# Summing the expert counts one background step later in the gates of the attention layer with experts

## The chip, the cores and the metric

The kernel runs on one core of one Trainium2 chip. The metric is the device time of one execution in microseconds (us), without the host. Three runs of the kernel before gave 539.40, 538.65 and 539.07 us; their median is 539.07 us.

## The reference

Three layers follow each other in fp32, on 4 batches of 576 positions: a linear attention, a layer in which two of four attention experts answer each position, and a layer of eight feed-forward experts.

```python
def _attn_ref(q, k, v, w_phi):              # layer 1: 8 heads, 128 features
    def phi(x):
        proj = np.einsum('bhsd,df->bhsf', x, w_phi)
        proj = proj - np.max(np.abs(proj), axis=-1, keepdims=True)
        return np.concatenate([np.exp(proj), np.exp(-proj)], axis=-1)
    q_p, k_p = (phi(q), phi(k))
    kv = np.einsum('bhsf,bhsd->bhfd', k_p, v)
    z = np.sum(k_p, axis=2)
    num = np.einsum('bhsf,bhfd->bhsd', q_p, kv)
    den = np.einsum('bhsf,bhf->bhs', q_p, z)[..., None] + 1e-06
    return (num / den).astype(np.float32)

def _moe_ref(x, w_gate, wq, wk, wv, wo):    # layer 2: E = 4 attention experts, K = 2
    logits = x @ w_gate
    topk = np.argpartition(-logits, K, axis=-1)[..., :K]
    sel = np.take_along_axis(logits, topk, axis=-1)
    w = np.exp(sel - sel.max(-1, keepdims=True))
    w /= w.sum(-1, keepdims=True) + 1e-09
    for e in range(E):
        q, k, v = x @ wq[e], x @ wk[e], x @ wv[e]
        ...                                 # causal softmax a of scale * q k^T
        ye = a @ v @ wo[e]
        for kk in range(K):
            out += (topk[:, :, kk] == e)[..., None] * w[:, :, kk:kk + 1] * ye

def _moe2_ref(x, w_gate, w_local, w1, w2):  # layer 3: E = 8, F = 1024
    ...                                     # each position keeps the expert of the one before, or takes a fresh one
    out[b, s] = p[e] * (np.maximum(x[b, s] @ w1[e], 0.0) @ w2[e])
```

## The kernel before

**Phase A** (class `PhaseA`) is layer 1. It runs 16 units (4 batches by 4 pairs of heads) in a software pipeline, by the list `A_STEPS`: `k`, `e`, `q` project keys and queries (tiles pjk, pje, pjq, line 267), `x` and `f` transpose and take exponentials, `kv` multiplies keys by values (Y, L335), `s` sums the keys (L344), `n0` and `n1` give the numerators (pn, L384), `d0` and `d1` in every second unit the denominators (pd, L401). `n0` is copied out of its accumulator by VectorE (DVE, L389), `n1` by ScalarE (ACT, L387), the denominators by DVE (L403).

**Phase B** (classes `PhaseB` and `Slot`) is layer 2. Each batch has a slot (s0, s1, s2, s3) for the two experts that its positions use most, and a fifth slot, x, takes one further expert. `B_STEPS` lists the steps of a slot: `s` scores (sc), `p` transposes, `v`, `o` the output projection (px, L64 to L66, copied out by ACT in L1238), `f` or `h` one of the next slot's (or its own remaining) projections (pq, twelve matmuls in L770). A projection's two halves are written by ACT as the high part (L735, two instructions) and subtracted by DVE as the low part (L737, two instructions); the values' half is copied by ACT alone (L753). **Phase C** is layer 3.

**The gates of layer 2** (`Gates.top2`, line 535) run once for each batch, as a generator in the background queue (class `Background`). A `t` in a step list is a tick, and a tick takes one step of the first entry of each lane; the gates are in lane "r". A bare `yield` ends a step and the next one comes with the next tick; `yield 2` lets one tick pass without a step, `yield 3` two. The steps of `top2` that matter here, each in terms of its lines:

- the counts: the selection `sel` (L557, L558), a memset (L559) and `cnt`, the sum over the five groups of positions (L561), on DVE;
- the sum of the counts over the partitions: a matmul with a matrix of ones (pc, L564; two matmul instructions of 4 columns), and in the same step five DVE instructions that scale the weights `w` (L565, L567 to L570);
- the total `tot`, which reads the matmul's accumulator on DVE (L574);
- the ranks (`by_use`, L522 and L524): how many experts have a larger total; then `hot` (L527), and then `perm` (L530, L532).

For the batches in turn, counted through the lists: the first batch's counts stand in unit 9 after `f0`, its pc between `kv1` and `kv2`, its total after `kv3`. The second batch's pc stands in unit 13 between `z0` and `s0`, its total after `d1`. The third's pc stands at the first tick of slot s0, ahead of `s0a s0b h1`, its total after them. The fourth's pc stands in slot x ahead of `f f p0a`, its total after them.

**What sets the order.** The program text does not give the order on an engine by itself. A planner goes through the program with modelled times and gives each engine, whenever it comes free, the earliest instruction in the text that is ready in the model; the engines then run the order that came out. A step of the background queue may not be issued ahead of the anchors, the last marked instructions of the main work on the same engine (`Background.step`, `issue_after`). pc, pje, pn, pd, the gates' logits pg (L503), pq and px share one tag of accumulators, `mm`, with two buffers:

```python
            ps.same = {"tr": ("X", 5), "X": ("X", 5), "mm": ("mm", 2)}
```

A tile of the tag needs one of the two buffers, and a buffer comes free when the last reader of its tile is done; pc's last reader is `tot`.

Of the kernel before, what the change touches and what calls it, by code (L numbers as in the profile page):

```python
# [484 lines left out]
class Gates:  # L485
# [5 lines left out]
    def t(self, shape, tag, b, bufs=1, dt=F32):  # L491
        return self.wk.tile([128] + list(shape), dt, tag=tag, name=f"{tag}_{b}", bufs=bufs)
# [42 lines left out]
    def top2(self, xf, wg32, b, out):  # L535

        nc, k, t, ps = self.nc, self.k, self.t, self.ps
        L = t([QT, 4], "L4", b)
        nc.vector.memset(L[:, 4, :], 0.0)
        yield from self.logits(xf, wg32, 4, L, b)  # L540
        Le = L[:, :, :, None].to_broadcast([128, QT, 4, 4])
        Lf = L[:, :, None, :].to_broadcast([128, QT, 4, 4])

        mx = t([QT], "mx", b)
        nc.vector.tensor_reduce(mx, L, axis=AX.X, op=OP.max)
        w = t([QT, 4], "w4", b)
        nc.vector.tensor_tensor(w, L, mx[:, :, None].to_broadcast([128, QT, 4]), op=OP.subtract)
        nc.scalar.activation(w, w, AF.Exp)
        yield
        c1, c2 = t([QT, 4, 4], "c1", b), t([QT, 4, 4], "c2", b)  # L550
        nc.vector.tensor_tensor(c1, Lf, Le, op=OP.is_gt)
        nc.vector.tensor_tensor(c2, Lf, Le, op=OP.is_equal)
        nc.vector.tensor_tensor(c2, c2, k.lower[:, None, 0:4, 0:4].to_broadcast([128, QT, 4, 4]), op=OP.mult)
        nc.vector.tensor_tensor(c1, c1, c2, op=OP.add)
        yield
        sel = t([QT, 4], "sel", b)
        nc.vector.tensor_reduce(sel, c1, axis=AX.X, op=OP.add)  # L557
        nc.vector.tensor_scalar(sel, sel, 1.5, None, op0=OP.is_lt)  # L558
        nc.vector.memset(sel[64:128, 4, :], 0.0)  # L559
        cnt = t([4], "cnt4", b)  # L560
        nc.vector.tensor_reduce(cnt, sel.rearrange("p t e -> p e t"), axis=AX.X, op=OP.add)  # L561
        yield 2
        pc = ps.tile([128, HALF], F32, tag="mm", name=f"pc_{b}")
        nc.tensor.matmul(pc[:, 0:4], k.ones, cnt, start=True, stop=True)  # L564
        nc.vector.tensor_tensor(w, w, sel, op=OP.mult)  # L565
        sm = t([QT], "sm", b)
        nc.vector.tensor_reduce(sm, w, axis=AX.X, op=OP.add)  # L567
        nc.vector.tensor_scalar(sm, sm, 1e-9, None, op0=OP.add)
        nc.vector.reciprocal(sm, sm)
        nc.vector.tensor_tensor(w, w, sm[:, :, None].to_broadcast([128, QT, 4]), op=OP.mult)  # L570
        yield
        tot = t([4], "tot4", b)

        nc.vector.scalar_tensor_tensor(tot, pc[:, 0:4], 8.0, k.iota[:, 0:4], op0=OP.mult, op1=OP.subtract)  # L574
        yield
        yield from self.by_use(tot, 4, b)
        hot, perm = self.hot, self.perm
        yield

        t4 = t([QT, 4, 4], "c1", b)  # L580
        nc.vector.tensor_tensor(t4, w[:, :, None, :].to_broadcast([128, QT, 4, 4]),
                                hot[:, None, :, :].to_broadcast([128, QT, 4, 4]), op=OP.mult)
        ws = t([QT, 4], "ws", b, 4)
        nc.vector.tensor_reduce(ws, t4, axis=AX.X, op=OP.add)
        out.update(ws=ws, perm=perm, hot=hot, tot=tot)
        yield
# [1209 lines left out]
```

## Time and profile before

| | |
|---|---|
| median of three runs | 539.07 us |
| the profiled execution's own time | 539.2 us |
| its span, first to last instruction | 537.0 us |
| TensorE matmul (PE) busy | 515.2 us (96%) |
| VectorE (DVE) busy | 359.2 us (67%) |
| ScalarE (ACT) busy | 264.9 us (49%) |
| GpSimd (POOL) busy | 150.2 us (28%) |

The profile is one execution. PE is TensorE's matmuls, PEld its weight loads. A line of the timeline gives the start, the time covered, the engine, the line of the kernel with its operation and tiles, and the count; in brackets stand idle time of the engine just ahead and what ended it. Lines of one kind that follow each other are merged.

### The profile page before, as it was taken

The page shows a single profiled execution, that of the slowest core. Times are in us where ns is not written, and L with a number is a line of the kernel's source. Part 1 is how long each engine was busy: PE and PEld are TensorE (multiplying, and loading weights), DVE is VectorE, ACT ScalarE, POOL GpSimd, SP SyncE. Part 2 cuts the span into 40 slices and gives each one's busy share as a digit, 9 for nine tenths or more (in the row PEclk, how much of TensorE's full clock was granted, in tenths as well). Part 3 has the DMA queues.
Part 4 walks back from the last instruction along what each step waited for, and adds up shares of the span by engine and source line. Part 5 has one row for each costly group of instructions (what it writes and reads, how often), then busy time and mean ns, then how long its engine had stood idle before and what let it go on. Part 6 is the DMA issues. An engine that isn't in the chain of part 4 may idle for free.

```text
span 537.0 us, 11793 instructions
## 1 busy us (share of the span) xinstructions
PE 515.2 (96%) x4456; PEld 435.4 (81%) x4456; DVE 359.2 (67%) x968; ACT 264.9 (49%) x607; POOL 150.2 (28%) x254
## 2 busy tenths in 40 slices
PE   7999999999999999999899899999999999999995
PEld 5776765666666787778677798999999999999995
DVE  7776777878863787877897965742764366617541
ACT  3857566565665467867748455331451235115100
POOL 5674696398467141212016100000000000000000
PEclk9999999999999999999999999999999999999998
DMA  8433364444116024602003202081435133813011
GB/s 249 134 98 105 108 215 126 149 147 164 28 44 212 9 69 131 196 2 81 1 0 139 100 1 69 13 287 75 134 144 169 46 129 123 282 48 128 2 57 38
DMA packets 32709, 57.07 MB, mean 106 GB/s; under 512 B 7012, under 2 KB 17636, under 8 KB 31620
## 3 DMA queue, kind: packets, MB, share of 16 engines
q1 hardware_dynamic: 32644, 56.24, 32.2%
q8 instruction: 37, 0.61, 0.5%
q14 instruction: 28, 0.23, 0.1%
HBM read 41.86 MB, written 14.36 MB: 105 GB/s over the span
## 4 chain that ended last, share of the span: by engine, by line
PE 83%; DVE 9%; ACT 4%; DMA 1%; issue 1%; SPq 0%; POOL 0%; DVEq 0%; ACTq 0%; POOLq 0%
PE po_c L64 6%; PE po_c L65 6%; PE po_c L66 6%; PE ph_c L64 6%; PE ph_c L65 6%; PE pq_s L770 6%; PE ph_c L66 6%; PE Y L335 6%; PE pn L384 5%; PE pd L401 3%; PE pjk L267 3%; PE py_s L917 2%; PE pt_s L889 2%; PE tr L321 2%; PE pjq L267 2%; PE pg L503 2%
## 5 line engine op out<-in xcount | busy, mean ns | idle before, releaser
L1478 ACT ACTIVATE h_c<-ph_c 128x288 fp32r<-128x288 f32 x64 | 26.0, 410 | 104.0 <-PE ph_c L66 103.9
L64 PE MATMUL ph_c<-xh_c,w1h_c 128*128 128x288 f32 x256 | 76.9, 301 | 0.0
L64 PE MATMUL po_c<-h_c,w2h_c 128*128 128x288 f32 x256 | 76.1, 297 | 0.0
L65 PE MATMUL po_c<-h_c,w2h_c 128*128 128x288 f32 x256 | 75.5, 295 | 0.0
L65 PE MATMUL ph_c<-xl_c,w1h_c 128*128 128x288 f32 x256 | 75.5, 295 | 0.0
L66 PE MATMUL po_c<-h_c,w2l_c 128*128 128x288 f32 x256 | 75.4, 295 | 0.0
L66 PE MATMUL ph_c<-xh_c,w1l_c 128*128 128x288 f32 x256 | 75.3, 295 | 0.0
L311 POOL TENSOR_TENSOR zs<-a_kp 128x256 f32<-128x256 f32 x64 | 48.2, 766 | 51.8 <-ACT a_kp L307 25.9
L1479 DVE SCALAR_TENSOR_TENSOR h_c<-ph_c,h_c 128x288 fp32r<-128x288 f32 x64 | 28.6, 452 | 34.5 <-ACT h_c L1478 34.2
L64 PEld LDWEIGHTS ph_c<-xh_c,w1h_c 128*128 128x128 f32 x256 | 48.1, 188 | 1.9 <-issue 0.9
L64 PEld LDWEIGHTS po_c<-h_c,w2h_c 128*128 128x128 f32 x256 | 48.1, 188 | 0.9 <-issue 0.9
L65 PEld LDWEIGHTS ph_c<-xl_c,w1h_c 128*128 128x128 f32 x256 | 48.1, 188 | 0.0
L66 PEld LDWEIGHTS po_c<-h_c,w2l_c 128*128 128x128 f32 x256 | 48.1, 188 | 0.0
L66 PEld LDWEIGHTS ph_c<-xh_c,w1l_c 128*128 128x128 f32 x256 | 48.0, 188 | 0.1
L65 PEld LDWEIGHTS po_c<-h_c,w2h_c 128*128 128x128 f32 x256 | 48.1, 188 | 0.0
L770 PE MATMUL pq_s<-xh_b,w_s 128*128 128x288 f32 x192 | 43.5, 304 | 0.7 <-DVE b_kz L737 0.3
L1501 DVE TENSOR_TENSOR fo_c<-po_c,pb 128x288 f32<-128x288 f32 x32 | 14.5, 454 | 44.3 <-PE po_c L66 44.2
L335 PE MATMUL Y<-a_kp,a_v 128*64 128x256 f32 x320 | 38.9, 384 | 0.4
L384 PE MATMUL pn<-qp,kvs 128*64 128x288 f32 x256 | 34.6, 408 | 0.3 <-ACT qp L371 0.3
L306 ACT ACTIVATE a_kp<-uk 128x1024 f32<-128x1024 f32 x30 | 31.6, 1052 | 6.4 <-PE tr L321 3.5
L770 PEld LDWEIGHTS pq_s<-xh_b,w_s 128*128 128x128 f32 x192 | 32.0, 188 | 3.4 <-issue 1.4
L323 ACT ACTIVATE qp<-tr 128x512 f32<-128x512 f32 x64 | 33.6, 631 | 1.4 <-PE tr L321 1.4
(315 smaller groups left out, 1199.0 us busy)
## 6 DMA issues: line engine op xcount, KB each, us to landing
w1raw_c<-in_w_dram SPq DMA_DIRECT2D x16, 512.0 KB, 4.2
w2raw_c<-in_w_dram SPq DMA_DIRECT2D x16, 512.0 KB, 4.7
raw<-in_kq_dram SPq DMA_DIRECT2D x15, 320.0 KB, 3.1
rb<-d SPq DMA_DIRECT2D x32, 144.0 KB, 3.2
x1d<-x SPq DMA_DIRECT2D x4, 1152.0 KB
x2d<-x SPq DMA_DIRECT2D x4, 1152.0 KB
raw<-in_kq_dram SPq DMA_DIRECT2D x16, 256.0 KB, 3.8
a_v<-in_v_dram SPq DMA_DIRECT2D x16, 256.0 KB, 3.8
```

Source lines behind the costliest of these rows:

```text
L64: nc.tensor.matmul(out, lh, rh, start=start, stop=False, **kw)
L65: nc.tensor.matmul(out, lh, rl, start=False, stop=False, **kw)
L66: return nc.tensor.matmul(out, ll, rh, start=False, stop=stop, **kw)
L267: mm = one(nc.tensor.matmul(pt[h][:, 128 * t:128 * t + 128], raws[p, c:c + 128], w[p], start=True, stop=True))
L306: nc.scalar.activation(kp[:, 0:4, sg, :], u[:, 0:4, :], AF.Exp, scale=sc)
L311: add(zs[:, j, sg, :], kp[:, j, sg, :], kp[:, 2 + j, sg, :], op=OP.add)
L323: self.bg.anchor(nc.scalar.activation(qp[:, h, sg, 0:512], tp, AF.Exp, scale=sc))
L335: self.kv_last = one(nc.tensor.matmul(Y[64 * h:64 * h + 64, 0:256], vt[:, t, h, :], kp[:, t, :, h * NF:(h + 1) * NF], start=t == 0, stop=t ...
L384: one(nc.tensor.matmul(pn[64 * h:64 * h + 64, :], kvs[:, sg, 64 * h:64 * h + 64], qp[:, h, sg, c], start=sg == 0, stop=sg == 1))
L770: self.nc.tensor.matmul(out, self.wqkv[t][:, wj, ch, 0:m], x[:, ch, c], start=wj == ch == 0 and x is xh, stop=wj == 1 and ch == 3)
L1478: nc.scalar.activation(hh[:, c], ph, AF.Relu),
L1479: nc.vector.scalar_tensor_tensor(hl[:, c], ph, 0.0, rd(hh[:, c]), op0=OP.max, op1=OP.subtract))
```

## The change

The step with the matmul pc and the five weight instructions comes one tick later, and the bare `yield` between the total and the ranks is gone, so that both are one step. All later steps of the gates stay at their ticks.

```diff
@@ class Gates, def top2
         cnt = t([4], "cnt4", b)
         nc.vector.tensor_reduce(cnt, sel.rearrange("p t e -> p e t"), axis=AX.X, op=OP.add)
-        yield 2
+        yield 3
         pc = ps.tile([128, HALF], F32, tag="mm", name=f"pc_{b}")
         nc.tensor.matmul(pc[:, 0:4], k.ones, cnt, start=True, stop=True)
         nc.vector.tensor_tensor(w, w, sel, op=OP.mult)
...
         tot = t([4], "tot4", b)
 
         nc.vector.scalar_tensor_tensor(tot, pc[:, 0:4], 8.0, k.iota[:, 0:4], op0=OP.mult, op1=OP.subtract)
-        yield
         yield from self.by_use(tot, 4, b)
         hot, perm = self.hot, self.perm
         yield
```

## Rows read from the trace of the kernel before

**Rows 1.** The page: the chain that ended last, shares by engine.
```profile
PE 83%; DVE 9%; ACT 4%; DMA 1%; issue 1%; SPq 0%; POOL 0%; DVEq 0%; ACTq 0%; POOLq 0%
```

**Rows 2.** Instructions on pc: idle time before them, us and times, by releaser.
```profile
  DVE cnt L561: 3.3, 4
```

**Rows 3.** PE's timeline in unit 9, first batch's gates.
```profile
79.65 0.69 PE L503 MATMUL pg<-x,b_wg 128*32 128x288 f32 x8
80.27 2.16 PE L384 MATMUL pn<-qp,kvs 128*64 128x288 f32 x16
82.36 0.69 PE L503 MATMUL pg<-x,b_wg 128*32 128x288 f32 x8
...
91.06 0.72 PE L267 MATMUL pjk<-a_w,raw 64*128 64x128 f32 x8
92.89 0.38 PE L564 MATMUL pc<-cnt,ones 128*128 128x4 f32 x2 [1.11 <-DVE cnt L561]
93.20 2.16 PE L384 MATMUL pn<-qp,kvs 128*64 128x288 f32 x16
96.04 2.15 PE L401 MATMUL pd<-qp,kvs 128*32 128x288 f32 x32 [0.68 <-DVE x L389]
```

**Rows 4.** DVE's timeline, the same stretch.
```profile
91.83 0.66 DVE L558 TENSOR_SCALAR sel<-sel 128x20 f32<-128x20 f32 x1
92.65 0.19 DVE L561 TENSOR_REDUCE cnt<-sel 128x4 f32<-128x20 f32 x1
93.31 0.16 DVE L574 SCALAR_TENSOR_TENSOR tot<-pc,iota 128x4 f32<-128x4 f32 x1
95.55 0.44 DVE L389 COPY x<-pn 128x288 f32<-128x288 f32 x1
```

**Rows 5.** Timeline of unit 13, second batch's gates.
```profile
136.39 1.14 PE L384 MATMUL pn<-qp,kvs 128*64 128x288 f32 x8
137.48 0.36 PE L564 MATMUL pc<-cnt,ones 128*128 128x4 f32 x2
138.47 0.39 ACT L387 ACTIVATE x<-pn 128x288 f32<-128x288 f32 x1
138.55 2.15 PE L401 MATMUL pd<-qp,kvs 128*32 128x288 f32 x32
```

**Rows 6.** Timeline of slot s0's start, third batch's gates.
```profile
181.34 0.39 PE L564 MATMUL pc<-cnt,ones 128*128 128x4 f32 x2 [0.33 <-DVE cnt L561]
181.41 0.17 DVE L567 TENSOR_REDUCE sm<-w 128x5 f32<-128x20 f32 x1
181.76 0.16 DVE L574 SCALAR_TENSOR_TENSOR tot<-pc,iota 128x4 f32<-128x4 f32 x1 [0.18 <-PE pc L564]
181.84 0.16 DVE L568 TENSOR_SCALAR sm<-sm 128x5 f32<-128x5 f32 x1
183.69 0.41 ACT L753 ACTIVATE pb_vT_s<-pq_s 128x288 f32<-128x288 f32 x1 [4.87 <-PE pq_s L770]
```

**Rows 7.** Timeline from slot x's start, fourth batch's gates.
```profile
241.45 0.29 PE L66 MATMUL px_s<-yh_s,wol_s 128*128 128x288 f32 x1
241.58 0.28 PE L564 MATMUL pc<-cnt,ones 128*128 128x4 f32 x2
242.11 0.40 PE L770 MATMUL pq_s<-xh_b,w_s 128*128 128x288 f32 x1
242.28 0.74 DVE L825 TENSOR_REDUCE nmx_x<-sc_x 64x1 f32<-64x576 f32 x1
244.01 0.83 ACT L735 ACTIVATE q_s<-pq_s 64x288 fp32r<-64x288 f32 x2
244.87 0.92 DVE L737 SCALAR_TENSOR_TENSOR q_s<-pq_s,q_s 64x288 fp32r<-64x288 f32 x2
245.94 0.37 PE L770 MATMUL pq_s<-xh_b,w_s 128*128 128x288 f32 x1
246.99 0.92 DVE L737 SCALAR_TENSOR_TENSOR q_s<-pq_s,q_s 64x288 fp32r<-64x288 f32 x2 [0.29 <-ACT q_s L735]
248.06 0.37 PE L770 MATMUL pq_s<-xh_b,w_s 128*128 128x288 f32 x1 [0.17 <-DVE q_s L737]
250.75 0.37 PE L770 MATMUL pq_s<-xh_b,w_s 128*128 128x288 f32 x1 [0.32 <-DVE b_kz L737]
```

## The prediction

> **What bounds the kernel now.** I read the page's shares of the chain first: 83% of the span's end is set by PE, 9% by DVE, 4% by ACT [rows 1]. A change pays only where PE stands still, or where DVE or ACT holds the chain. Next come the instructions on pc: PE and its loads sat 3.3 us, in 4 waits, for the counts [rows 2]. That figure counts a weight load and its matmul both. In the timelines the matmul itself waited 1.11 us in the first batch [rows 3] and 0.33 us in the third [rows 6]; in the second and fourth the row of pc has no bracket [rows 5, 7], so PE came to it without waiting. What the change aims at is thus 1.11 + 0.33 = 1.44 us, 0.27% of 539.2 us. Last I read what stands on PE, DVE and ACT around each of the four, since a step moved in the text is moved on the chip only if the planner's order changes.
>
> **How the order can change.** Two facts from the rows. First, text order does not bind PE: in unit 9 half of unit 10's key projection (91.06) was issued ahead of pc (92.89), though it stands behind pc in the text [rows 3]. Second, tiles of the two-buffer tag mm do come in text order wherever I can see it. In unit 8 the text has the first half of the logits, then n0 and n1, then the second half; PE ran 79.65, 80.27 and 82.36 in that order. In unit 9 the numerators ran right behind pc, at 93.20, although PE had stood idle for 1.11 us [rows 3]. I therefore take the order of mm tiles in the text as the order on PE, and ask for each batch which mm tiles lie between the old and the new place.
>
> **First batch.** The new place is behind kv2 and kv3 instead of ahead of them. These use no mm tile, and they were already issued long before pc: counts ended at 92.65 + 0.19 = 92.84, which is what pc waited for [rows 4]. So pc still comes ahead of n0 and n1, and still waits. The total moves behind n0's copy in the text, but it was ready at 93.31, and that copy came at 95.55 [rows 4]. The anchors are the same on both ticks. Term: 0. The other end is the whole wait, -1.11, should the planner let the numerators pass. Nothing here can lose, since no main instruction is moved behind another.
>
> **Second batch.** pc moves behind s0, d0 and d1, so the denominators take the two buffers first. Today PE runs n1, pc, sums, half a projection and pd without a gap (136.39, 137.48, 138.55) [rows 5]; afterwards the same work in another order, also without one. The second denominator needs the buffer of n1, which ACT frees at 138.47 + 0.39 = 138.86 [rows 5]. pd could now begin some 0.6 us sooner, so its first half would end near 138.55 - 0.6 + 2.15/2 = 139.0, just behind that copy. DVE's later total costs 0.16 and the ranks about the same twice, in a stretch where the chain is PE's. Term: 0, ends -0.2 and +0.3 (a planner that counted on an earlier copy than 138.86).
>
> **Third batch.** Here the chain runs through the counts. pc moves behind s0a, s0b and one projection of twelve matmuls. PE, instead of waiting 0.33 us, goes on with scores and the projection, and the counts are ready long before pc: -0.33. The new cost is in the buffers. The projection and pc then hold both, so the next projection must wait until the total has read pc or ACT has copied the projection out. Today the total ends 181.76 + 0.16 - 181.34 = 0.58 us behind the start of pc, and pc itself takes 0.39, leaving 0.19 us of wait; ACT's copy takes 0.41 [rows 6]. Scores that could fill it are not ready. So -0.33 + 0.19 = -0.14, and I take -0.15. Ends: -0.33 (filled) and +0.3 (the total comes behind another DVE instruction).
>
> **Fourth batch.** pc moves behind two projections of slot s2 (f f). Today the first of them starts at 242.11, 0.66 us behind the start of the last output matmul (241.45); pc (241.58 to 241.86) and its total lie between, with score matmuls as filler [rows 7]. ACT writes the projection's high part at 244.01 and the chain then goes ACT, DVE to the projections at 245.94, 248.06 and 250.75; the last two wait 0.17 and 0.32 us for DVE [rows 7]. If the first projection starts at the end of the step of 241.45, it starts at 241.58, so 242.11 - 241.58 = 0.53 us is the most that can be won. Against it: pc now waits for the first projection's buffer, free after DVE's subtraction (244.87 + 0.92 = 245.79 today), and the third projection waits for pc (0.28) and the total (wait and read, 0.35 as in the third batch). From 245.79 - 0.53 this is 245.26 + 0.28 + 0.35 = 245.89, against 245.94 today: even. Behind that, ACT and DVE have the earlier start of the two projections, and the filler scores with their exponentials come later, so that half of the 0.53 is used up again. Term: -0.2. Ends: -0.5, and +1.2 (below, the slower rival).
>
> **The weight instructions and the ranks.** The five instructions on `w` are lower in the text by a tick, but they wait only for the selection and run in DVE's free time today (181.41 and 181.84 around the total) [rows 6]; 0. Ranks, `hot` and `perm` feed weight loads many ticks later; no DMA is moved across a tick, and SP and POOL issue what they issued. 0. Their cover is the time to the next slot; were it gone, a wait of the same 1 to 4 us by which the total is late would show in the loads, which I see no sign of.
>
> **The sum.** 0 + 0 - 0.15 - 0.2 = -0.35 us. From the profiled 539.2 us this is 538.85; that execution was 0.13 us above the median of 539.07, so on the median 538.7 us.
>
> **Rivals.**
>
> *The numerators pass (or the planner reorders unit 9 otherwise).* Then the 1.11 us goes too, and pd, which waited a further 0.68 us for n0's copy, itself behind the gate's instructions on DVE [rows 3, 4], comes up to that much sooner. Sum: 539.07 - 0.35 - 1.11 - 0.68/2 = 537.3 us; both waits gone in full would be 536.9. For it: the wait is on the chain. Against it: the order of the mm tiles is the same in the text as before. Chance 0.17.
>
> *The total blocks DVE (slower).* Place: fourth batch. If the planner sets the total on DVE ahead of work that the chain needs, and pc is later than its model has it, DVE stands still; if it sets the total behind the score maximum (0.74) or the second projection's subtraction (0.92) [rows 7], the third projection waits for that. Price: both, 0.74 + 0.92 = 1.66, less the 0.49 of slack that today's waits (0.17 + 0.32) show: +1.2 us; with the same in the third batch (+0.3) 539.07 + 1.5 = 540.6. It decides from the point at which the third projection starts later than 245.94 + 0.5. For it: in the third batch DVE waited 0.18 for pc while the weight instruction whose input was there at 181.58 began only at 181.84 [rows 6]. Against it: in all four batches the total now follows pc within 0.6 us. [...] Chance 0.17.
>
> *The order shifts elsewhere.* From the third batch on the planner sees other times, and any later tie can fall differently, by tenths of a microsecond each, either way. With about 140 us of phase B behind it this makes -1 to +1 us. Half of it is inside 0.2%; chance of more than that 0.14, evenly split.
>
> **Chances.** The forecast itself has 0.52, with a range of its own of 538.0 to 539.4 us; the rivals 0.17, 0.17 and 0.14. 0.2% (1.08 us) is about what a measurement of this kernel can tell from no change. Faster by more than that: 0.17 and 0.07, 0.24 and a little of the forecast's edge: 0.25. Slower: most of 0.17, and 0.07: 0.2. The rest, 0.55, is within 0.2%. The range for 8 times in 10 goes from the first rival's 537.0 to 540.4, short of the slower rival's end.
>
> **What would show it.** In the first batch pc still waits about 1.1 us and the numerators follow it: right; pn ahead of pc: the first rival. In the second, pd ahead of pc with no bracket on either. In the third, pc behind twelve pq matmuls with no wait for the counts, and a wait of about 0.2 us on the next projection for the total or ACT's copy. In the fourth, the first projection near 241.6 less the shift so far, and pc behind the second one. DVE rows with a bracket "PE pc" above 0.5 us, or a third projection later by over 0.5 us, would speak for the slower rival. That mm tiles keep the text's order is the assumption that would bring all four terms down if it is wrong.

## The result, and the profile after

The changed kernel takes 541.43 us (median of 6 runs, 540.87 to 542.34) against 539.1 us: ratio 1.0051, 95% interval [1.0041, 1.0062]. By the medians it is 2.3 us slower, by the interval 2.2 to 3.3. The ratio is formed without the one slow run of before, 572.08 us. The forecast was 538.7 us and the range ended at 540.4, so sign and size were both wrong.

From line 575 on, a line of the changed kernel has a number lower by one. The profiled execution of after is 0.55 us ahead of that of before from its first units on, where nothing is changed; the other traces of this study begin between 0.66 us ahead and 0.32 behind. A difference between the two traces is therefore to be read against -0.55, not against 0. The page's chain of the end, shares by engine:

```profile
PE 76%; DVE 12%; ACT 4%; DMA 3%; issue 2%; POOL 1%; SPq 1%; ACTq 0%; POOLq 0%; DVEq 0%
```

PE's share fell from 83% [rows 1] to 76%, and VectorE's rose from 9% to 12%: more of the end is set by something for which PE waits. The instructions on pc, idle time before them and who waited for them:

```profile
  DVE cnt L561: 2.4, 2
  PE pc L564: 1.3, 2
...
who waited for it (us, times):
  DVE tot L574: 1.3, 2
```

The wait for the counts went from 3.3 us in 4 places [rows 2] to 2.4 us in 2, which is the third batch's wait gone (matmul and weight load are counted both). In its place VectorE waits 1.3 us for pc, in two batches.

**First batch.** The timeline of PE in unit 9:

```profile
92.33 0.39 PE L564 MATMUL pc<-cnt,ones 128*128 128x4 f32 x2 [1.11 <-DVE cnt L561]
92.65 2.16 PE L384 MATMUL pn<-qp,kvs 128*64 128x288 f32 x16
95.47 2.15 PE L401 MATMUL pd<-qp,kvs 128*32 128x288 f32 x32 [0.66 <-DVE x L389]
```

This is [rows 3] again, 0.56 us earlier throughout: the same order and the same 1.11 us.

**Second batch.** The timeline of unit 13, PE, DVE and POOL:

```profile
137.14 2.39 PE L401 MATMUL pd<-qp,kvs 128*32 128x288 f32 x32
...
139.46 0.39 PE L564 MATMUL pc<-cnt,ones 128*128 128x4 f32 x2
...
139.62 0.74 POOL L311 TENSOR_TENSOR zs<-a_kp 128x256 f32<-128x256 f32 x1
...
140.16 2.30 DVE L522 TENSOR_TENSOR u<-tot 128x16 f32<-128x16 f32 x1
...
140.31 0.73 POOL L313 TENSOR_TENSOR zs<-zs 128x256 f32<-128x256 f32 x1
...
141.00 0.74 POOL L311 TENSOR_TENSOR zs<-a_kp 128x256 f32<-128x256 f32 x1
...
141.69 0.74 POOL L312 TENSOR_TENSOR zs<-zs,a_kp 64x256 f32<-64x256 f32 x1
...
144.60 0.63 PE L321 MATMUL tr<-ident,uq 128*128 128x128 f32 x4 [1.42 <-DVE uk L276]
```

The same comparison in before, and GpSimd's first additions there:

```profile
138.07 0.17 DVE L522 TENSOR_TENSOR u<-tot 128x16 f32<-128x16 f32 x1
...
138.40 1.49 POOL L311 TENSOR_TENSOR zs<-a_kp 128x256 f32<-128x256 f32 x2 [5.59 <-PE Y L344]
```

pd runs ahead of pc, and neither has a bracket, as forecast. But the ranks' comparison (L522) takes 2.30 us instead of 0.17, and ends at 142.46, as GpSimd's addition of 141.69 does (142.43). VectorE's next key product (uk) is late by that, and PE waits 1.42 us for it. This trace drew a long one: in the four other traces with this batch changed the comparison takes 1.60 to 1.65 us, and unit 14 is 0.7 us late instead of 1.4.

**Third batch.** The timeline from slot s0's start:

```profile
183.37 0.28 PE L564 MATMUL pc<-cnt,ones 128*128 128x4 f32 x2
...
183.69 0.16 DVE L574 SCALAR_TENSOR_TENSOR tot<-pc,iota 128x4 f32<-128x4 f32 x1 [0.76 <-PE pc L564]
```

pc comes behind the projection and without a bracket. VectorE waits 0.76 us for it; PE waits for nothing until 190.83, and there for 0.16 us.

**Fourth batch.** The timeline from slot x's start; L819 and L822 are products and mask of slot x's scores, P_x its exponential, rw_x and by_x its row weights, py_x and px_x its attention and output products, pg the next logits of a gate (layer 3):

```profile
241.32 0.30 PE L66 MATMUL px_s<-yh_s,wol_s 128*128 128x288 f32 x1
...
241.46 0.29 PE L769 MATMUL pq_s<-xh_b,w_s 128*128 128x288 f32 x1
...
245.18 0.36 PE L564 MATMUL pc<-cnt,ones 128*128 128x4 f32 x2 [0.16 <-DVE q_s L736]
...
245.57 0.16 DVE L574 SCALAR_TENSOR_TENSOR tot<-pc,iota 128x4 f32<-128x4 f32 x1 [0.54 <-PE pc L564]
...
245.79 0.40 PE L769 MATMUL pq_s<-xh_b,w_s 128*128 128x288 f32 x1
...
249.99 0.37 PE L769 MATMUL pq_s<-xh_b,w_s 128*128 128x288 f32 x1 [0.54 <-DVE b_kz L736]
...
253.58 0.29 PE L819 MATMUL sc_x<-b_kz,q_x 128*64 128x288 f32 x1
253.71 0.19 PE L822 MATMUL sc_x<-cmaskr,ident 128*64 128x64 f32 x1
...
254.72 0.73 ACT L828 ACTIVATE P_x<-sc_x,nmx_x 64x576 f32<-64x576 f32 x1 [0.53 <-DVE nmx_x L824]
...
256.11 0.15 DVE L851 TENSOR_TENSOR rw_x<-rw_x,wsel_x 64x1 f32<-64x1 f32 x1
...
256.34 0.69 POOL L854 TENSOR_SCALAR by_x<-rw_x 64x64 f32<-64x64 f32 x1 [5.66 <-DVE rw_x L851]
257.08 0.30 PE L865 MATMUL rwt_x<-ident,by_x 128*64 128x128 f32 x1 [0.59 <-POOL by_x L854]
...
263.35 0.37 PE L1017 MATMUL px_x<-yl_x,woh_x 128*128 128x288 f32 x1 [1.28 <-DVE yl_x L1010]
...
270.69 0.69 PE L503 MATMUL pg<-x,c_wg 128*32 128x288 f32 x8
```

The same timeline of before, rows that were not shown (L820 and L823 are the same two score matmuls; the row of 217.69 is for the third batch, further down):

```profile
217.69 0.40 PE L770 MATMUL pq_x<-xh_x,w_x 128*128 128x288 f32 x1 [0.61 <-ACT x L1238]
...
241.72 0.32 PE L820 MATMUL sc_x<-b_kz,q_x 128*64 128x288 f32 x1
241.88 0.19 PE L823 MATMUL sc_x<-cmaskr,ident 128*64 128x64 f32 x1
...
260.50 0.37 PE L1018 MATMUL px_x<-yl_x,woh_x 128*128 128x288 f32 x1 [0.54 <-DVE yl_x L1011]
...
268.90 0.69 PE L503 MATMUL pg<-x,c_wg 128*32 128x288 f32 x8
```

The projections come earlier, as forecast: the first at 241.46 against 242.11, the last shown at 249.99 against 250.75 [rows 7]. But two score matmuls that before filled PE's wait between pc and the first projection, at 241.72 and 241.88, are issued at 253.58 and 253.71, behind six projections of twelve matmuls. Everything that hangs on them is a chain of small steps (maximum, exponential, row weight, GpSimd's spreading, transpose, py_x), and px_x starts at 263.35 instead of 260.50. At the logits of 270.69 the lag is +1.79, and then to the end +2.25. Counted from its own start of -0.55, this trace loses 1.4 us by unit 14, has won back 1.0 of it by slot x's start (lag -0.13), and loses 2.4 from there to the end.

### The profile page after: what moved, and what is told of

Same layout as the page of the kernel before. It is cut to its first block, busy times and chain, and to the rows that moved or that the text cites. A ratio compares the mean times of both kernels' runs of the same rounds, so it can differ in the third digit from the quotient of the medians.

```text
span 539.1 us, 11786 instructions
## 1 busy us (share of the span) xinstructions
PE 515.3 (96%) x4456; PEld 434.7 (81%) x4456; DVE 363.1 (67%) x968; ACT 265.3 (49%) x607; POOL 150.2 (28%) x254
## 4 chain that ended last, share of the span: by engine, by line
PE 76%; DVE 12%; ACT 4%; DMA 3%; issue 2%; POOL 1%; SPq 1%; ACTq 0%; POOLq 0%; DVEq 0%
PE po_c L64 6%; PE po_c L65 6%; PE po_c L66 6%; PE ph_c L64 6%; PE ph_c L65 6%; PE ph_c L66 6%; PE Y L335 5%; PE pn L384 4%; PE pq_s L769 4%; PE pjk L267 3%; PE pd L401 2%; PE py_s L916 2%; PE pt_s L888 2%; PE pg L503 2%; PE tr L321 2%
```

## The experiments

Theory 1: the loss is the two score matmuls, which lose their slot when PE's wait goes. Theory 2: the loss is the second batch, VectorE's comparison beside GpSimd's additions. The runs were timed in three groups, with before at 538.74, 538.6 and 538.67 us, and each difference is against before of its own group. Their intervals are 0.5 to 0.9 us to either side, so differences of some tenths between two runs say nothing.

**The fourth batch alone.** `cnt4` to pc: 3 steps, and total with ranks, only for b == 3.

```diff
-        yield 2
+        yield {3: 3}.get(b, 2)
...
-        yield
+        if b not in (3,):
+            yield
```

> The change in the fourth batch's gates alone. Theory 1 (the scores that filled PE's wait): with pc gone from the start of slot x, the last score matmuls of that slot fall behind five projections, and its output projection starts about 2.9 us later; the whole loss is here, +1.8 to +2.6 us on the kernel before, 541.3. Theory 2 (DVE held up by POOL in the second batch): the loss is not here, within 0.5 us of the kernel before.

Measured: 541.38 us (540.68 to 541.54), ratio 1.0045 [1.0032, 1.0058]. That is +2.64, as much as the whole change. The two scores again come behind six projections, and px_x starts at 263.16 with a 1.27 us wait.

**All batches but the fourth.** The same edit for b of 0, 1 and 2.

> The change in the first three batches, the fourth as before. Theory 1: 538.6 to 539.5, since the second batch's loss (1.4 us by the end of unit 13) is taken back by the third batch and by waits for transfers. Theory 2: 540.5 to 541.5, nearly the whole loss.

Measured: 538.63 us (537.64 to 539.12), 0.9991 [0.9982, 1.0001]; the two score matmuls are back at 241.85 and 242.02. The first three batches together change nothing that can be measured, although the comparison takes 1.65 us here. Theory 2 can't be the whole loss.

**Only the two score matmuls moved.** Before, with no edit of the gates; in slot x the two are held until the fifth projection of the next slot has been issued (`pqs` lists the projections' last matmuls).

```diff
+                late = last and nm == "x" and i == 4 and e == es[-1]
+                with self.owner.bg.tc.issue_after(self.owner.pqs[-2].ins) if late else nullcontext():
+                    nc.tensor.matmul(out, self.q2[:, e, s0:s0 + sn], self.kz[:, e, k0:k1], start=False, stop=not last)
+                    if last:
...
```

> The kernel before, with all four batches' gates as before, and one thing changed: the last two score matmuls of slot x (second product of the last 64 positions and the mask) are held until the fifth projection of the next front is issued, where the whole change had put them; the total of the counts stays ahead of the first projection. Theory 1 (the loss is these two matmuls, which no longer fill TensorE's wait): 540.7 to 541.7 us, the two at about 253.5, px_x from about 263.2 with a wait of some 1.3 us on yl_x, against 260.5 before. Rival (the loss is the later counts: the total, the ranks and the weights of the fourth batch come 3 us later, or pc among the projections holds a buffer): 538.5 to 539.5 us, as before, with px_x below 261.

Measured: 541.92 us (540.53 to 543.33), 1.0056 [1.0039, 1.0072], +3.3 us. Its timeline of PE:

```profile
241.57 0.28 PE L565 MATMUL pc<-cnt,ones 128*128 128x4 f32 x2
242.11 0.40 PE L771 MATMUL pq_s<-xh_b,w_s 128*128 128x288 f32 x1 [0.26 <-DVE tot L575]
...
253.66 0.29 PE L824 MATMUL sc_x<-b_kz,q_x 128*64 128x288 f32 x1
253.80 0.19 PE L827 MATMUL sc_x<-cmaskr,ident 128*64 128x64 f32 x1
...
263.44 0.37 PE L1022 MATMUL px_x<-yl_x,woh_x 128*128 128x288 f32 x1 [1.28 <-DVE yl_x L1015]
```

As in the whole change the two come behind the sixth projection. That late scores cost the whole loss is shown: with pc in its old place, and no other edit, these two instructions (under 0.5 us of PE) make px_x 2.94 us late. The sizes agree by the traces: from the last output product ahead of slot x to the end, the lag grows by 2.4 us here, by 2.4 in the whole change and by 2.6 in the fourth batch alone (3.3 and 2.64 by the medians, whose intervals overlap). The whole change had its first projection 0.52 us sooner (241.46 against 242.11, less the 0.13 by which its trace was ahead one row earlier), and nothing of that is left at px_x.

**The scores ahead, with the change.** Slot x's four remaining scores stand ahead of the projections in its list.

```diff
-    "x": ("s0a t f f p0a t t t s1a t f f f t t t s2a t p1a s3a ... p3a f s4a t n1 ...
+    "x": ("s0a t s1a s2a s3a s4a f f p0a t t t t f f f t t t t p1a ... p3a f t n1 ...
```

> The whole change, and in slot x's list the four later score steps moved ahead of the projections (s1a s2a s3a s4a before f f). Theory 1: the last scores are done near 242 us again, the output projection of slot x starts near 260 us, and the time is 538.3 to 539.5. Theory 2: 541.0 to 541.6, as with the change alone.

Measured: 540.35 us (539.53 to 541.67), 1.0031 [1.0021, 1.0041]; px_x at 261.40. Better than the change by about 1.1 us, but not as good as expected.

**The same list without the change.**

> Control for the run that had slot x's four remaining scores ahead of the projections together with the change: here the same list without the change. That run came out at 540.35 us, 1.2 above before. If the list itself costs (the scores' exponentials and weight products collide with ScalarE and VectorE work of slot s1's end): 539.8 to 540.8 us here too, and the change on top of it is worth nothing. If the list costs nothing and the change keeps 1.2 us of loss in another way than by the scores: 538.4 to 539.3 us.

Measured: 540.17 us (539.73 to 541.34), 1.0028 [1.0019, 1.0037]. The list itself costs 1.6 us: PE then comes to slot x's transposes before GpSimd and VectorE have the row weights, and waits 0.23 and 0.73 us for them. With this list the whole change is worth 540.35 - 538.74 = 1.61 against 540.17 - 538.6 = 1.57, nothing. So early scores do take the change's loss away, but this way of having them early costs as much.

**The change, with pc in another tag.** For the fourth batch pc's tile is of tag tr (the transposes') instead of mm.

```diff
-        pc = ps.tile([128, HALF], F32, tag="mm", name=f"pc_{b}")
+        pc = ps.tile([128, 512 if b == 3 else HALF], F32, tag="tr" if b == 3 else "mm", name=f"pc_{b}")
```

> The whole change with the fourth batch's counts in a PSUM tile of the transposes' tag: the counts' matmul stays ahead of the first projection and holds no buffer of the projections, but the last two score matmuls of slot x are still issued only after the last projections. Theory 1 (the scores are the loss): 540.7 to 542.0 us, px_x from about 263. Rival (the loss is the counts' matmul between the second and third projection): 538.3 to 539.3 us.

Measured: 540.42 us (540.22 to 540.93), 1.0034 [1.0022, 1.0047]. pc is back ahead of the projections, the two score matmuls are still at 253.03 and 253.16, px_x at 262.80. So pc among the projections is not the loss; the time was 0.3 us under the range of theory 1.

**Before, with pc in that tag.**

> All four gates as before, but the fourth batch's counts are summed into a PSUM tile of the transposes' tag instead of the projections' tag, so that the first projection needn't wait until VectorE has read the total, and the scores of slot x keep their early places (nothing is queued behind a held buffer). Theory 1: the 0.53 us wait in slot x goes without moving the scores back: 538.2 to 538.9 us, px_x from about 260.0 to 260.5. Rival (each gain of half a microsecond there is lost again, or the two transposes that need the tag come late): 538.9 to 540.0 us.

Measured: 538.53 us (538.07 to 539.42), 0.9994 [0.9985, 1.0003]. The wait is gone (first projection at 241.77), the scores all come ahead of pc, and px_x starts at 260.06; this trace was 0.17 us ahead at slot x's start. What the wait itself is worth, with its cover kept, is too little to be measured (0.2 us by the trace). And it corrects theory 1 in one point: the wait goes here too, and the scores come earlier, at 240.27 and 240.40, while in the run before this one pc stands ahead of the projections without a wait, too, and they come late. That the wait's going sends them back is thus not shown. What is shown is what their lateness costs; why the planner's order has them there stays open, as its modelled times are not on record.

**Fewer additions on GpSimd beside the second batch.** The whole change, and in unit 13 one addition per sign in place of four.

```diff
-            for j in range(2):
+            for j in range(1 if i == 13 else 2):
                 add(zs[:, j, sg, :], kp[:, j, sg, :], kp[:, 2 + j, sg, :], op=OP.add)
+            if i == 13:
+                continue
```

> The whole change, and in unit 13 alone POOL does one add of the key sums in place of four for each sign (the sums of three of the five groups of positions are left out, so the denominators of that unit are not the reference's). Theory 2: the comparison of the second batch's totals takes 0.17 us in place of 2.30, PE's wait of 1.42 us in unit 14 goes, and the time falls to 539.1 to 540.0. Theory 1: the comparison gets as short, but the time stays at 541.0 to 541.6, since that loss is taken back before slot x.

Measured: 540.43 us (539.65 to 541.8), 1.0033 [1.0021, 1.0045]. VectorE's timeline:

```profile
139.91 0.15 DVE L576 SCALAR_TENSOR_TENSOR tot<-pc,iota 128x4 f32<-128x4 f32 x1
140.09 0.18 DVE L524 TENSOR_TENSOR u<-tot 128x16 f32<-128x16 f32 x1
```

At the same time as in the whole change the same comparison takes 0.18 us: GpSimd's two additions had run from 137.46 to 138.91. PE's wait for the key product is gone. So GpSimd's additions are what holds the comparison up. (The sums of three of the five groups of positions are left out, so the denominators of unit 13 are wrong.) The time, 1.0 us under the whole change, puts the mechanism's worth at some 0.6 to 1 us of the 2.3 (1.69 over before here, 2.33 there).

**The second batch alone.** The edit of the first run with `b == 1`.

> The change in the second batch alone. Theory 2 (the rank comparison is held up by GpSimd's additions and TensorE waits for VectorE's next key product): a rank comparison of 1.6 to 2.3 us in unit 13 and the key transposes after it 0.8 to 1.4 us late there. If that loss reaches the end: 539.5 to 540.6 us. If the slack between the third gate and slot s1's second projections takes it back, as the run with all batches but the fourth suggests: 538.2 to 539.2 us.

Measured: 539.41 us (538.47 to 540.58), 1.0014 [1.0005, 1.0023], +0.74. From its timeline:

```profile
140.69 1.61 DVE L522 TENSOR_TENSOR u<-tot 128x16 f32<-128x16 f32 x1
...
144.45 0.63 PE L321 MATMUL tr<-ident,uq 128*128 128x128 f32 x4 [0.73 <-DVE uk L276]
```

The lag against before (both traces start together here) is +0.71 in unit 14 and +0.44 from slot x's start on. Part is taken back, most reaches the end; the time lies between the two expected ranges.

**The third batch alone.** The same with `b == 2`.

> The change in the third batch alone. TensorE no longer waits 0.5 us for the counts at slot s0's start, and the slot starts 0.3 to 0.8 us earlier. If that reaches the end: 537.7 to 538.3 us. If it is taken back before slot x, as gains and losses ahead of it were in the runs so far: 538.3 to 539.2 us.

Measured: 537.47 us (536.95 to 538.37), 0.9981 [0.9972, 0.9990], -1.20. This was better than either expectation. Relative to its own start (0.49 us early) the trace is 0.6 us ahead in the projections at 184, level at 207, and 0.8 us ahead at the logits of 226.72. The 0.61 us wait of the row at 217.69 is not there. The saved wait was 0.33 us. The wait at 217.69, for ScalarE's copy of x, is there with 0.32 to 0.64 us in all six traces whose third gate is as before, and in none of the eight in which it is changed. The two add up to 0.7 to 1.0 us, and this trace ends 0.75 us further ahead than it started. Why slot x's first projection no longer waits, nothing run here separates.

**First and third batch.** The third as above; for the first pc is asked for two steps later (`yield 4`) and `hot` shares the ranks' step, so that n0 and n1 pass pc.

> Second and fourth batch as before. Third batch as changed; first batch with the total of the counts asked for two steps later and the expert choice in the step of the total and the ranks, so that the numerators of unit 9 pass the counts' matmul and only the key product waits. The rival of the prediction for the first batch gave 0.9 us less there; the third batch showed 0.83 us less by the fourth slot's start, of which little was left at the end. If what is won early reaches the end: 537.2 to 538.2 us. If early gains are taken back later, as in the run with all batches but the fourth: 538.4 to 539.3 us.

Measured: 539.17 us (536.29 to 541.01), 1.0003 [0.9987, 1.0019], not to be told from before although the third batch alone won 1.2. The runs scatter, so the time settles little; the trace, which loses 0.9 us between units 9 and 13, says why nothing was won. DVE's timeline in unit 9:

```profile
94.73 0.66 DVE L531 TENSOR_TENSOR u<-hot,iota 128x16 f32<-128x16 f32 x1
95.32 2.88 DVE L583 TENSOR_TENSOR c<-w,hot 128x80 f32<-128x80 f32 x1
98.12 0.15 DVE L533 TENSOR_REDUCE perm<-u 128x4 f32<-128x16 f32 x1
98.23 0.24 DVE L586 TENSOR_REDUCE ws<-c 128x20 f32<-128x80 f32 x1
```

PE's wait of 1.11 us became 0.16, and the gate's products lie beside GpSimd's additions (93.92 to 99.59, no gap over 0.1 us). One takes 2.88 us, the copy of the denominators is queued behind it, and PE waits 1.91 us at 99.00. In before the same product, beside additions too, was quick:

```profile
95.31 0.23 DVE L581 TENSOR_TENSOR c<-w,hot 128x80 f32<-128x80 f32 x1
```

**The third batch as changed, the fourth in the other tag, the rest as before.**

> A version to beat both: the third batch as changed, the fourth batch's order as before but its counts in a PSUM tile of the transposes' tag, which took 0.3 us off slot x in the last run of it. If both pay: 537.5 to 538.3 us; if only the tag pays: 538.2 to 538.8 us; if a score matmul of slot x is moved back by the third batch's shift: above 539.5 us.

Measured: 537.44 us (537.0 to 538.43), 0.9980 [0.9971, 0.9989]. It beats both kernels, by 1.2 and by some 3.6 us (541.43 - 539.1 is 2.33, and 538.67 - 537.44 is 1.23). The third batch alone does as well, so the tag adds nothing that shows.

## Why the prediction was wrong

| batch | forecast | ends | alone, measured |
|---|---|---|---|
| first | 0 | -1.11 to 0 | order and wait unchanged |
| second | 0 | -0.2 to +0.3 | +0.74 |
| third | -0.15 | -0.33 to +0.3 | -1.20 |
| fourth | -0.2 | -0.5 to +1.2 | +2.64 |
| sum | -0.35 | | +2.18 (whole: +2.33) |

The first batch was not run alone; its entry is the whole change's trace. The terms add up to what the whole change does, as near as terms known to half a microsecond can, so nothing points to one acting on another.

**Right.** Tiles of tag mm keep the text's order: pn behind pc in the first batch, pd ahead of pc in the second, pc behind one projection in the third and two in the fourth. The first batch gains nothing. In the fourth the first projection follows the last output product by 0.14 us, one matmul's step (0.13 to 0.14 us in the projection that follows), and the third comes at 245.79 where the working gave 245.89. The slower rival's deciding point, a third projection behind 246.44, was not reached. DVE did wait for pc 0.76 and 0.54 us, over the 0.5 that was to speak for that rival, and it cost nothing that shows: that sign was badly chosen. The first rival's 1.11 us, of the numerators passing pc, was no gain at hand either: in the one run where the order was made so, the wait moved behind the denominators.

**Wrong: the fourth batch, the step on the filler.** The working found the score matmuls in PE's wait, counted them as filler, and took "half of the 0.53" for their coming later. It never asked how much later, nor who waits for them. They did not come later by the length of the wait. Their next place in the planner's order was behind six projections, 12 us on, although PE stood idle for 0.54 us on the way there (249.99), and a chain over four engines hangs on them, 9.8 us from 253.58 to px_x. In place of -0.2 the term is +2.64, and the two matmuls late by themselves cost as much. One row held the warning: the score maximum nmx_x at 242.28, right behind the two [rows 7], is on the way to px_x. The upper end of +1.2 was priced from the projections' buffers, which is another mechanism.

**Wrong: the second batch, "the ranks about the same twice".** Their durations were taken from a place where GpSimd stands still (0.17 us at 138.07), and put where it adds without a gap. A row that should have made me look was among those shown: L558, 128x20 values in 0.66 us in unit 9, with others of 0.16 and 0.19 beside it [rows 4]. In place of about 0.16 us the comparison took 1.60 to 2.30, and the term is +0.74. The run with fewer additions shows that GpSimd's additions are the cause: with none beside it the same comparison took 0.18 us. One addition takes 0.71 to 0.74 us in this unit in the traces with the long comparison. In unit 9 of before the first gate's TENSOR_TENSOR instructions, beside additions too, take 0.16 to 0.60 us, less than one. But 1.60 us is two additions and more, and 2.30 and 2.88 us are three and more, so the instruction ended behind additions that had started after it: in the whole change those of 140.31, 141.00 and 141.69 all end ahead of the comparison begun at 140.16. By what rule the two engines hold each other up was not shown.

**Wrong in size: the third batch.** The sign held and the wait of 0.33 us went, but -1.20 is beyond the forecast's end. The 0.19 us that the working set against it did not come either: scores that it took for not ready filled the place behind pc (183.51 to 183.94). What was left out is the second wait, of 0.32 to 0.64 us at slot x's first projection (217.69), which goes with it. That a shift can change later ties by tenths either way stood among the rivals with both signs; that it added to the gain here is luck.

## What to carry to other kernels

A wait on the busiest engine may be the slot in which a planner places work that others wait for. Before taking the wait away, list what runs in it, follow each item to its users, and find the next place that the planner would give it. And take a small instruction's duration from a row with the same neighbours on the other engines, not from wherever it was quick.

## What was not expected of the hardware

A comparison of 128x16 values on VectorE took 0.17 us alone and, beside GpSimd's additions, 1.60 to 1.65 us in four traces and 2.30 in one; a product of 128x80 took 2.88 us in one trace and 0.23 in another, both beside additions. The long comparisons end within 0.04 us behind the end of an addition, the second or third that started after them. Reductions beside the same additions (L524, L533, L586) kept 0.14 to 0.24 us. What decides between one addition's length and several is open: no run varied the phase of the two engines by itself.

The wait ahead of px_x, 1.27 or 1.28 us, was followed by a fall of the granted clock in two of the five traces that have it. The granted clock by stretches of 2 us (columns: stretch, length, busy time of PE, PEld, DVE, ACT and POOL, clock, DMA share, GB/s), in the run of the fourth batch alone:

```profile
262.00:264.00 2.00, 0.77 (x4) 0.56 (x4) 1.83 (x5) 1.60 (x5) 0.09 (x1) 1.00 0.00 0
264.00:266.00 2.00, 1.71 (x7) 1.41 (x8) 1.94 (x5) 1.66 (x7) 0.00 (x0) 0.70 0.00 0
266.00:268.00 2.00, 2.00 (x10) 1.83 (x9) 1.35 (x3) 1.92 (x8) 0.00 (x0) 0.50 0.00 0
268.00:270.00 2.00, 2.00 (x16) 2.00 (x14) 2.00 (x4) 1.90 (x5) 0.00 (x0) 0.95 0.03 8
```

PE was busy 0.77 us of the first stretch, and the clock then fell to 0.70 and 0.50; in the last stretch, after 2.00 us of PE in the one before, it is 0.95. In the whole change's trace the same stretches, with 0.72 us of PE in the first, have 1.00 throughout, and so they have in the trace of the two scores alone. By the next logits the trace with the fall is 0.26 us later, counted from px_x. In the fourth batch alone they stand here:

```profile
270.76 0.69 PE L503 MATMUL pg<-x,c_wg 128*32 128x288 f32 x8
```

That is 7.60 us behind its px_x (263.16), against 7.34 in the whole change (263.35 to 270.69) and 7.34 with the two scores alone. The run with fewer additions had a fall to 0.50 too, and 7.62 us; the whole change with the other tag had none, and 7.36.
